# Converting the w_in slices by visits, and products (0,0) and (0,1) one visit later, in a fused retention and SiLU kernel

## The chip, the cores and the metric

The kernel runs on one core of a Trainium2 chip. The metric is device time in microseconds from the first to the last of the program on that core; a time shown is the median of several runs. The engines of the core named here are TensorE (PE, with its weight loads as PEld), VectorE (DVE), ScalarE (ACT), GpSimd (POOL) and SyncE (SP), whose queue issues nearly all DMA transfers of this kernel. Each engine works through its own instructions in order.

## The reference

A recurrent retention layer feeds a two-layer network with SiLU. B=4, H=8, S=768, D=64; 3072 tokens of 512 numbers; w_in is 512 x 2048 and w_out 2048 x 512, both 64-bit floats.

```python
gamma = 1.0 - 2.0 ** (-5.0 - np.arange(H))
for t in range(S):
    state = gamma * state + outer(k[:, :, t], v[:, :, t])      # per batch and head, D x D
    y[:, :, t] = scale * q[:, :, t] @ state
x = y.transpose(0, 2, 1, 3).reshape(B * S, H * D)
h = x @ w_in
out = (h / (1 + exp(-h))) @ w_out
```

## The kernel before

**Chunks and units.** The sequence is cut into NC=6 chunks c of 128 steps; with the 4 batches b that makes 24 units n = 4c+b. Inside a chunk, retention is a masked product of scores; between chunks a state (D x D per head) is carried. `visit(m)` (L497) works on three units at once: it transposes k and q of unit m (`stage_t`, L353, with ACT copying the results out of PSUM), forms the scores and state sums of unit m-1 (`stage_s`, `stage_a`), and the output y of unit m-2 (`stage_y`, L409). On DVE `finish_a` (L390) multiplies the scores by the decay mask ("am", L394) and updates the state (L403, L407), `scale_q` (L348) and `scale_k` (L330) scale q and k; for units 8 to 13 k's scaling is done on ACT in two halves of four heads. `finish_y` (L445) copies y out (L454) and `split_x` (L459) cuts it into three parts of limited precision for PE: the first on ACT (L466), two on DVE (L469, L470).

**Products.** `product_in(c, f)` (L535) multiplies chunk c's x (512 columns, four units) by slice f of w_in (128 of its 2048 columns): 8 matrix instructions into "ha", 4 into "hb". ACT copies ha out (L543), DVE subtracts hb (L547), ACT applies Silu (L551), and `put_g` (L554) sends the result g to DRAM one product later. The three PSUM banks "h" that hold ha and hb are shared with the transposes of k. Copies of y and the g tiles share three buffers "hs".

**Slices of w_in.** A slice arrives as 64-bit words (`load_w`, L153, two buffers "wf"). `convert_w` (L172) turns it into 32-bit numbers: one ACT instruction (L193) and six on DVE (L195 to L210, the last in `rounded`). `split_w` (L111) cuts the result into three parts: ACT (L117), DVE (L120), ACT (L122), DVE (L123). `take_w` (L218) does this for the next slice in number; with parts=1 the end of it is put behind the subtraction of the next product (list `behind_next`), with parts=2 the conversion and the first step of `split_w` are put there and the remaining three steps behind the mask of the next visit (list `behind_mask`, emptied in `visit`). Converting slice i also asks for the load of slice i+2, which waits until slice i's buffer has been read.

**What sets the order.** The order on PE is the order of the program, written out by hand at the end of the kernel (L608 to L662). The order on the other engines, and that of SP's transfers, is made when the kernel is built, by a planner that goes by priority (place in the program) and by its own estimate of when each instruction is ready; `tc.issue_after(x)` makes the instructions in its block follow x on x's engine. `taken_out[0]` is the latest product's subtraction, `masked[0]` the latest mask, `copied[0]` the latest copy of ha, `evac[0]` the latest copy of transposed k or q. Once a first product has run, `finish_a` is put behind `taken_out[0]` (in `visit`).

**The order before, around the change.** Visits 0 to 3; slice 0 taken; visits 4 and 5; slice 1 taken behind visit 5's mask; visit 6; product (0,0); visit 7; the load of slice 3; visit 8; product (0,1); slice 2 taken with parts=2; visit 9. Then the list `steps`: (1,0), visit 10, (1,1), visit 11, (0,2), (1,2), visit 12, (0,3), (1,3), visit 13, (0,4), (1,4), (2,0), (0,5) and so on. The slices 3 to 9 are taken after (1,0), (0,2), (0,3), (0,4), (0,5), (0,6), (0,7).

Exp is used on ACT for the decays of `chunk_decays` and `first_chunk` at visit 0; its first Silu is that of product (0,0).

Of the kernel before, what the change touches and what calls it, by code (L numbers as in the profile page):

```python
# [15 lines left out]
AF = mybir.ActivationFunctionType  # L16
# [15 lines left out]
def kernel(  # L32
# [27 lines left out]
    nc = tc.nc  # L60
    B, H, S, D = q.shape
# [11 lines left out]
    scale = 1.0 / math.sqrt(D)  # L73
# [37 lines left out]
    def split_w(f, w32, name, factor, to):  # L111


        to[f] = w = w_slot(f, name)
        lo = conv.tile([128, 512], FP32, tag="wl", name=f"{name}l_{f}")
        with tc.issue_after(held[0] if f >= NF - 4 else evac[0]):
            nc.scalar.activation(out=w[:, 0, :], in_=w32, func=AF.Copy, scale=HALF * factor)  # L117
        high = w[:, 0, :].bitcast(FP32)
        yield
        nc.vector.scalar_tensor_tensor(out=lo, in0=w32, scalar=factor, in1=high,  # L120
                                       op0=ALU.mult, op1=ALU.subtract)
        nc.scalar.activation(out=w[:, 1, :], in_=lo, func=AF.Copy, scale=1.0 / EPS)  # L122
        nc.vector.scalar_tensor_tensor(out=w[:, 2, :], in0=high, scalar=EPS, in1=lo,  # L123
                                       op0=ALU.mult, op1=ALU.subtract)
# [4 lines left out]
    EARLY = 2 * B  # L129
    early = {}  # L130

    def load(name, n):
        if n >= len(units):
            return
        c, b = units[n]
        src = {"k": k, "q": q, "v": v}[name]
        if n < EARLY:

            if n not in early:
                early[n] = wpool.tile([128, 3, H, D], FP32, tag=f"w{4 + n}", name=f"kqv_{n}")  # L140
            t = early[n][:, "kqv".index(name)]
        else:
            t = ld.tile([128, H, D], FP32, tag=f"{name}f", name=f"{name}f_{n}",
                        bufs=2 if name == "q" else 3)
        nc.sync.dma_start(out=t, in_=src[b, :, ds(c * C, C)].rearrange("h t d -> t h d"))  # L145
        kqv[name][n] = t
# [68 lines left out]
    evac, held, w_sb = [], [], {}  # L215
    taken = [0]

    def take_w(after=None, parts=0):  # L218


        i = taken[0]
        taken[0] += 1
        if i >= 2 * NF:
            return
        with tc.issue_after(after) if after else ExitStack():
            rounded = convert_w(i)

        def finish():
            w32 = rounded()
            if i < NF:  # L230
                split = split_w(i, w32, "wi", scale, w_sb)
                if parts == 2:
                    next(split)
                    behind_mask.append(split)
                else:
                    list(split)
            else:
                nc.sync.dma_start(out=wo_dram[i - NF], in_=w32)

        if parts:  # L240
            behind_next.append(finish)
        else:
            with tc.issue_after(after) if after else ExitStack():
                finish()

    W_AHEAD = 2
    for n in range(EARLY):
# [17 lines left out]
    for j in range(2):  # L265
        for a in range(HP):
            nc.scalar.activation(out=decay[:, j, a, :], in_=lag[:, :D], func=AF.Exp,
                                 scale=float(lg[2 * a + j]))
# [5 lines left out]
    lgc = const.tile([128, HP], FP32, tag="lgc", name="lgc")  # L274
# [16 lines left out]
    def first_chunk():  # L291
        nc.gpsimd.iota(lag, pattern=[[1, C]], base=1, channel_multiplier=0,
                       allow_small_or_imprecise_dtypes=True)
        for a in range(HP):
            nc.scalar.activation(out=gq[:, a, :], in_=lag, func=AF.Exp, scale=lgc[:, a : a + 1])

    def next_chunk():
        for a in range(HP):
            nc.scalar.activation(out=gq[:, a, :], in_=gq[:, a, :], func=AF.Copy,
                                 scale=step[:, a : a + 1])  # L300


    xt, kt, qt, am = {}, {}, {}, {}
    behind_next, behind_mask, behind_copy = [], [], []
    taken_out, copied, masked = [], [], []
    state, steps_of = {}, {}

# [13 lines left out]
    token = const.tile([1, 1], FP32, tag="token", name="token")  # L321
# [8 lines left out]
    def scale_k(n):  # L330
        if 0 <= n < len(units):
            t = kqv["k"][n]
            if units[n][0] == NC - 1:
                t = t[:D]
            if 2 * B <= n < 3 * B + 2:

                def half(heads):
                    for h in heads:
                        nc.scalar.activation(out=t[:, h, :], in_=t[:, h, :], func=AF.Copy,
                                             scale=gk[:, units[n][0], h : h + 1])  # L340

                half(range(H // 2))
                behind_copy.append(lambda: half(range(H // 2, H)))
                return
            g = gk[: t.shape[0], units[n][0], :].unsqueeze(2).to_broadcast([t.shape[0], H, D])
            nc.vector.tensor_tensor(out=t, in0=t, in1=g, op=ALU.mult)
# [150 lines left out]
    def visit(m):  # L497

        first, mid, last = (0 <= m - i < len(units) for i in range(3))
        if first:  # L500
            stage_t(m)
        if last:
            scores, states_with, yp = stage_y(m - 2)
            scores()
        if mid:
            sc, sums = score_tile(m - 1)
            stage_s(m - 1, sums)
        if last:
            states_with(0)
        if mid:  # L510
            stage_a(m - 1, sc)
            if m > 1 and units[m - 1][1] == 0:
                next_chunk()
            with tc.issue_after(taken_out[0]) if taken_out else ExitStack():
                finish_a(m - 1, sc, sums)
            with tc.issue_after(masked[0]):
                while behind_mask:
                    list(behind_mask.pop(0))
            scale_q(m - 1)
        if m == 0:  # L520
            chunk_decays()
            first_chunk()
        if first:
            scale_k(m)
        if last:
            states_with(1)
            finish_y(m - 2, yp)
        for name, n in (("k", m + 2), ("q", m + 2), ("v", m + 1)):
            if n >= EARLY:
                load(name, n)  # L530


    pending = []

    def product_in(c, f):  # L535
        ha, hb = turn(f"ha_{c}_{f}"), turn(f"hb_{c}_{f}")
        for i in range(3):
            for kk in range(KIN):
                nc.tensor.matmul(hb if i == 2 else ha, lhsT=w_sb[f][:, i, ts(kk, 128)],  # L539
                                 rhs=xt[c][:, i, kk, :], start=kk == 0 and i != 1,  # L540
                                 stop=kk == KIN - 1 and i != 0)
        hs = hpool.tile([128, NT], FP32, tag="hs", name=f"g_{c}_{f}")
        copied[:] = [nc.scalar.activation(out=hs, in_=ha, func=AF.Copy, scale=ONE_E).ins]  # L543
        with tc.issue_after(copied[0]):
            while behind_copy:
                behind_copy.pop(0)()
        taken_out[:] = [nc.vector.tensor_tensor(out=hs, in0=hs, in1=hb, op=ALU.subtract).ins]  # L547
        with tc.issue_after(taken_out[0]):
            while behind_next:
                behind_next.pop(0)()  # L550
        nc.scalar.activation(out=hs, in_=hs, func=AF.Silu)  # L551
        pending.append((c, f, hs))
# [55 lines left out]
    for m in range(EARLY + 2):  # L608
        visit(m)
        if m == 3:  # L610
            take_w()
        elif m == 5:
            take_w(masked[0])
        elif m == EARLY - 2:
            product_in(0, 0)
        elif m == EARLY - 1:
            load_w(3)
        elif m == EARLY:
            product_in(0, 1)
            take_w(taken_out[0], 2)  # L620

    half = NF // 2
    pairs = [(1, 0), (1, 1)] + [(c, f) for f in range(2, 4) for c in range(2)]
# [4 lines left out]
            [(2, f) for f in range(half, NF)])  # L628
    groups = [(c, f) for c in range(3, NC) for f in range(NF)]
    steps = pairs + three + rest + last + groups  # L630
    takes = [(1, 0)] + [(0, f) for f in range(2, half)]
    takes += [(2, half - 4), (2, half - 2)]
    takes += [(0, half), (0, half + 2), (1, half), (1, half + 2)]
    takes += [(0, NF - 4), (0, NF - 2), (2, half + 2), (2, half + 4)]
    takes += [(c, f) for c in (3, 4) for f in (0, 3, 6, 8, 11, 14)]
    behind = {(1, f): lambda f=f: visit(EARLY + 2 + f) for f in range(4)}
    at = ([(1, NF - 1)] + [(2, f) for f in range(NF - 7, NF - 2, 2)] +
          [(c, 4 * i + 1) for c in range(3, NC - 1) for i in range(B)])
    for i, x in enumerate(at):
# [5 lines left out]
    for n, (c, f) in enumerate(steps):  # L645
        product_in(c, f)
        if (c, f) in takes:
            take_w(taken_out[0], 2 if n < len(pairs) else int(n < len(pairs + three)))
        put_g(1)
        behind.get((c, f), lambda: None)()  # L650
        if c == NC - 1:
            if f == 0:
                get_w(0)
                get_w(1)
            if f < NF - 4:
                w_out(f)
            if f >= NF - 6:
                if f == NF - 6:
                    for n in range(G_AHEAD):
                        get(n)  # L660
                if f >= NF - S_AHEAD:
                    split(f - NF + S_AHEAD)  # L662
    put_g(0)

    for c in range(NC):
# [8 lines left out]
        for f in range(NF):  # L674
            n = c * NF + f
# [62 lines left out]
```

## Time and profile before

| | us |
|---|---|
| median of 6 runs (636.47 to 640.79) | 639.14 |
| the profiled execution's own time | 640.48 |
| its span | 638.7 |
| PE busy in the span | 612.9 |
| DVE busy | 421.7 |
| ACT busy | 305.2 |

The profile is one execution. Its page gives totals, slices of the span and the costliest groups; the trace behind it can be asked for stretches of time (busy time of each engine, granted TensorE clock, share of the DMA engines), for what each engine waited for, and for the instructions in order of time. A row in order of time reads: start, duration, engine, line, operation, output<-input. Durations overlap a little: a 128x512 instruction on DVE shows 0.68 or 0.69 us, and the next starts 0.60 us after it began. Times in microseconds are from the start of the span.

### The profile page before, as it was taken

Reading aid. Unit: us, or ns where it says so; the run is one execution under the profiler, and the core shown is the slowest. Engines: PE = TensorE matmul, PEld = TensorE weight load, DVE = VectorE, ACT = ScalarE, POOL = GpSimd, SP = SyncE. Lnnn points to the kernel's source line nnn. Section 1 sums busy time; section 2 is a strip of 40 time slices with the busy share of each in tenths; the row PEclk is TensorE's granted clock in tenths of the full one; section 3 lists DMA queues with packets and bytes.
Section 4 is the critical chain, followed back from the end, with each engine's and each line's share of the span. In section 5 each row is a group of like instructions: output and inputs, shape, how many; then the busy total and the mean of one; then the engine's idle time right before and its main releaser. Section 6 shows DMA issues by size and latency. Waiting matters only on the chain.

```text
span 638.7 us, 13560 instructions
## 1 busy us (share of the span) xinstructions
PE 612.9 (96%) x5440; PEld 507.1 (79%) x5440; DVE 421.7 (66%) x731; ACT 305.2 (48%) x590; POOL 7.3 (1%) x65
## 2 busy tenths in 40 slices
PE   5787999999999999999999999999999999999997
PEld 4676888887888888888887788888888888888785
DVE  2896899798977778687777766363544645554631
ACT  5675997666755555555467762231412221312311
POOL 3000000000000000000000000000000000000000
PEclk9998999999999999999999999999999999999999
DMA  9995877554677677774756643242342524332301
GB/s 202 204 218 121 225 211 240 173 165 158 208 214 186 195 239 214 211 232 166 231 192 214 201 153 107 91 166 98 133 131 78 186 67 132 132 123 88 120 0 67
DMA packets 123215, 103.65 MB, mean 162 GB/s; under 512 B 80016, under 2 KB 88464, under 8 KB 123152
## 3 DMA queue, kind: packets, MB, share of 16 engines
q1 hardware_dynamic: 120272, 97.54, 51.9%
q10 hardware_dynamic: 2880, 5.24, 2.2%
q8 instruction: 43, 0.70, 0.5%
q14 instruction: 20, 0.16, 0.1%
HBM read 66.06 MB, written 36.70 MB: 161 GB/s over the span
## 4 chain that ended last, share of the span: by engine, by line
PE 84%; DMA 4%; DVE 4%; ACT 3%; SPq 2%; issue 2%; ACTq 0%; DVEq 0%; POOLq 0%
PE ha L539 23%; PE o L687 20%; PE oa L687 13%; PE hb L539 12%; PE ob L687 7%; PE y L419 3%; DMA wf<-in_moe_w_in_dram 1%; DMA wr<-wod 1%; PE sc L376 1%; PE sc L386 1%; SPq L145 1%; PE qp L360 1%; PE kp L360 1%; DMA kqv<-in_q_dram 1%; DMA kf<-in_k_dram 1%
## 5 line engine op out<-in xcount | busy, mean ns | idle before, releaser
L539 PE MATMUL ha<-xt,wi 128*128 128x512 f32 x768 | 194.5, 396 | 1.8 <-ACT xt L466 1.8
L539 PEld LDWEIGHTS ha<-xt,wi 128*128 128x128 f32 x768 | 143.4, 189 | 33.1 <-ACT xt L466 2.0
L687 PE MATMUL o<-wo,gs 128*128 128x512 f32 x576 | 146.3, 389 | 0.0
L687 PEld LDWEIGHTS o<-wo,gs 128*128 128x128 f32 x576 | 108.2, 188 | 22.4
L596 DVE TENSOR_TENSOR gs<-gr,gs 128x512 fp32r<-128x512 f32 x96 | 62.2, 686 | 90.7 <-ACT gs L594 90.7
L687 PE MATMUL oa<-wo,gs 128*128 128x512 f32 x384 | 118.3, 389 | 0.0
L594 ACT ACTIVATE gs<-gr 128x512 fp32r<-128x512 f32 x96 | 53.4, 620 | 134.7 <-issue 132.3
L539 PE MATMUL hb<-xt,wi 128*128 128x512 f32 x384 | 104.6, 395 | 2.1 <-ACT g L543 2.1
L547 DVE TENSOR_TENSOR g<-g,hb 128x512 f32<-128x512 f32 x96 | 65.7, 685 | 46.4 <-ACT g L543 27.3
L539 PEld LDWEIGHTS hb<-xt,wi 128*128 128x128 f32 x384 | 72.9, 191 | 18.9 <-ACT g L543 3.5
L687 PEld LDWEIGHTS oa<-wo,gs 128*128 128x128 f32 x384 | 72.1, 188 | 15.0
L551 ACT ACTIVATE g<-g 128x512 f32<-128x512 f32 x96 | 60.7, 632 | 46.9 <-DVE g L547 46.5
L687 PE MATMUL ob<-wo,gs 128*128 128x512 f32 x192 | 75.3, 392 | 0.3 <-DVE o L696 0.3
L543 ACT ACTIVATE g<-ha 128x512 f32<-128x512 f32 x96 | 56.7, 591 | 35.7 <-PE ha L539 23.9
L597 DVE SCALAR_TENSOR_TENSOR gs<-gs 128x512 fp32r<-128x512 f32 x96 | 62.0, 685 | 0.0
L687 PEld LDWEIGHTS ob<-wo,gs 128*128 128x128 f32 x192 | 36.1, 188 | 9.3 <-DVE o L696 2.0
L193 ACT ACTIVATE ca<-wf 128x512 f32<-128x512 f32 x32 | 21.7, 677 | 11.1 <-DVE cs L200 5.1
L419 PE MATMUL y<-qt,mid 64*64 64x64 f32 x384 | 21.4, 226 | 2.1 <-issue 2.1
L394 DVE TENSOR_TENSOR am<-sc,decay 128x512 f32<-128x512 f32 x24 | 16.5, 687 | 9.9 <-PE sc L386 9.9
L200 DVE SCALAR_TENSOR_TENSOR cs<-ca,cs 128x512 uint32<-128x512 uint32 x32 | 22.1, 691 | 1.0
L204 DVE SCALAR_TENSOR_TENSOR cp<-wf,cp 128x512 f32<-128x512 uint32 x32 | 22.1, 690 | 0.7
L695 ACT ACTIVATE o<-o 128x512 f32<-128x512 f32 x10 | 6.0, 597 | 33.4 <-PE o L687 33.0
(79 smaller groups left out, 539.1 us busy)
## 6 DMA issues: line engine op xcount, KB each, us to landing
gd<-g SPq DMA_DIRECT2D x96, 256.0 KB, 3.1
gr<-gd SPq DMA_DIRECT2D x96, 256.0 KB, 2.7
wf<-in_moe_w_out_dram SPq DMA_DIRECT2D x16, 512.0 KB, 4.2
out_dram<-o ACTq DMA_DIRECT2D x20, 256.0 KB, 2.1
wf<-in_moe_w_in_dram SPq DMA_DIRECT2D x16, 256.0 KB, 4.2
wf<-in_moe_w_in_dram SPq DMA_DIRECT2D x32, 128.0 KB, 3.9
kf<-in_k_dram SPq DMA_DIRECT2D x16, 256.0 KB, 5.3
qf<-in_q_dram SPq DMA_DIRECT2D x16, 256.0 KB, 4.1
```

What stands on the lines that cost most here:

```text
L193: nc.scalar.activation(out=a.bitcast(FP32), in_=hi.bitcast(FP32), func=AF.Abs, scale=65536.0)
L200: nc.vector.scalar_tensor_tensor(out=s, in0=a, scalar=3, in1=s, op0=ALU.logical_shift_left, op1=ALU.bitwise_or)
L204: nc.vector.scalar_tensor_tensor(out=p.bitcast(FP32), in0=lo, scalar=2.0 ** -52, in1=p.bitcast(FP32), op0=ALU.mult, op1=ALU.mult)
L419: i = nc.tensor.matmul(yp[ts(e, D), o, a, :], lhsT=lhsT, rhs=rhs, start=(e, o) not in started, stop=True, skip_group_check=True).ins
L539: nc.tensor.matmul(hb if i == 2 else ha, lhsT=w_sb[f][:, i, ts(kk, 128)], rhs=xt[c][:, i, kk, :], start=kk == 0 and i != 1, stop=kk == KIN ...
L543: copied[:] = [nc.scalar.activation(out=hs, in_=ha, func=AF.Copy, scale=ONE_E).ins]
L547: taken_out[:] = [nc.vector.tensor_tensor(out=hs, in0=hs, in1=hb, op=ALU.subtract).ins]
L551: nc.scalar.activation(out=hs, in_=hs, func=AF.Silu)
L594: nc.scalar.activation(out=t[:, 0, :], in_=g, func=AF.Copy, scale=HALF)
L596: nc.vector.tensor_tensor(out=t[:, 1, :], in0=g, in1=high, op=ALU.subtract)
L597: nc.vector.scalar_tensor_tensor(out=t[:, 2, :], in0=t[:, 1, :].bitcast(FP32), scalar=-1.0 / EPS, in1=high, op0=ALU.mult, op1=ALU.add)
L687: nc.tensor.matmul(o, lhsT=g, rhs=wo[f][:, i, :], start=first_ and i != 1, stop=last and i != 0)
```

## The change

Slice 1 is converted from visit 6 and no longer from visit 5, and slices 2 to 6 from visits 8, 10, 11, 12 and 13 (`begin_w`, in `visit`, behind that visit's mask): the conversion and the first step of `split_w`. The remaining three steps (`end_w`) follow the mask of the next visit, or, for slice 6, the subtraction of the product after visit 13. Slices 7 and on are taken as before, so `take_w` needs no third kind of `parts`. `finish_a` is put behind the latest subtraction only for visits after 13. Products (0,0) and (0,1) follow visits 7 and 9; (0,0) still precedes visit 8 and (0,1) now directly precedes (1,0). The k of unit 8 is scaled by DVE in one instruction, no longer by ACT in eight. After the Exps of `first_chunk` a Silu of one element is added, whose result is not used.

```diff
-                split = split_w(i, w32, "wi", scale, w_sb)
-                if parts == 2:
-                    next(split)
-                    behind_mask.append(split)
-                else:
-                    list(split)
+                list(split_w(i, w32, "wi", scale, w_sb))
...
+    def end_w():
+        while half_split:
+            list(half_split.pop())
+
+    def begin_w():
+        i = taken[0]
+        taken[0] += 1
+        split = split_w(i, convert_w(i)(), "wi", scale, w_sb)
+        next(split)
+        half_split.append(split)
...
+        nc.scalar.activation(out=token, in_=lgc[:1, :1], func=AF.Silu)
...
-            if 2 * B <= n < 3 * B + 2:
+            if 2 * B < n < 3 * B + 2:
...
-            with tc.issue_after(taken_out[0]) if taken_out else ExitStack():
+
+            with tc.issue_after(taken_out[0]) if m > 3 * B + 1 else ExitStack():
                 finish_a(m - 1, sc, sums)
-            with tc.issue_after(masked[0]):
-                while behind_mask:
-                    list(behind_mask.pop(0))
             scale_q(m - 1)
...
+        if EARLY - 2 <= m < 3 * B + 2:
+            with tc.issue_after(masked[0]):
+                end_w()
+                if m not in (EARLY - 1, EARLY + 1):
+                    begin_w()
...
-        elif m == 5:
-            take_w(masked[0])
-        elif m == EARLY - 2:
-            product_in(0, 0)
         elif m == EARLY - 1:
             load_w(3)
-        elif m == EARLY:
+            product_in(0, 0)
+        elif m == EARLY + 1:
             product_in(0, 1)
-            take_w(taken_out[0], 2)
...
-    takes = [(1, 0)] + [(0, f) for f in range(2, half)]
+    takes = [(0, f) for f in range(5, half)]
...
-    behind = {(1, f): lambda f=f: visit(EARLY + 2 + f) for f in range(4)}
+    behind = {(1, f): lambda f=f: visit(EARLY + 2 + f) for f in range(3)}
+    behind[1, 3] = lambda: [visit(3 * B + 1), behind_next.append(end_w)]
...
-            take_w(taken_out[0], 2 if n < len(pairs) else int(n < len(pairs + three)))
+            take_w(taken_out[0], n < len(pairs + three))
```

EARLY is 8, B is 4 and `half` is 8.

## The prediction

> **What bounds the kernel now.** I read the page's totals first, then a table of stretches, the waits of one stretch, and the order of work on each engine from 33 to 100 us. PE is busy for 612.9 of 638.7 us, so only a pause of PE costs time. In the table of stretches the columns after the length are busy time and count of PE, weight loads, VectorE (DVE), ScalarE (ACT) and POOL, then granted clock, DMA share and GB/s.
>
> ```profile
> 42.00:44.00 2.00, 1.71 (x52) 1.40 (x44) 2.00 (x5) 1.76 (x3) 0.09 (x1) 1.00 0.74 154
> 44.00:46.00 2.00, 0.23 (x14) 0.25 (x17) 2.00 (x5) 1.99 (x4) 0.00 (x0) 1.00 0.85 209
> 46.00:48.00 2.00, 1.52 (x104) 1.39 (x98) 1.97 (x4) 2.00 (x7) 0.00 (x0) 1.00 0.92 235
> 48.00:50.00 2.00, 0.62 (x39) 0.48 (x30) 1.81 (x5) 0.71 (x2) 0.09 (x1) 1.00 0.95 182
> 50.00:52.00 2.00, 1.30 (x5) 1.04 (x6) 0.35 (x2) 0.96 (x2) 0.00 (x0) 0.90 1.01 225
> 52.00:54.00 2.00, 2.00 (x6) 1.51 (x6) 1.38 (x2) 1.13 (x4) 0.00 (x0) 0.50 0.21 46
> ...
> 58.00:60.00 2.00, 0.63 (x28) 0.36 (x20) 1.97 (x5) 1.97 (x7) 0.20 (x1) 1.00 0.40 93
> 60.00:62.00 2.00, 1.45 (x6) 1.23 (x7) 1.97 (x4) 0.50 (x1) 0.00 (x0) 0.96 0.54 166
> 62.00:64.00 2.00, 2.00 (x6) 1.51 (x6) 0.08 (x1) 0.69 (x2) 0.00 (x0) 0.50 0.81 217
> ```
>
> At 44 to 46 us DVE and ACT are full and PE nearly empty; from 52 to 54 and 62 to 64 us PE is full but at half clock. What ended PE's pauses from 36 to 66 us (waiter, what it waited for; total, times, longest):
>
> ```profile
> PE y L419 <- issue: 2.1, 1, 2.1
> PE y L419 <- ACT ys L454: 2.1, 1, 2.1
> PE ha L539 <- ACT xt L466: 1.8, 1, 1.8
> PE sc L376 <- DVE state L407: 0.5, 1, 0.5
> ```
>
> Why they are there stands in the order on DVE and ACT:
>
> ```profile
> 43.13 0.68 DVE L123 SCALAR_TENSOR_TENSOR wi<-wi,wil 128x512 fp32r<-128x512 f32 x1
> 43.74 0.68 DVE L547 TENSOR_TENSOR g<-g,hb 128x512 f32<-128x512 f32 x1
> 44.33 0.69 DVE L346 TENSOR_TENSOR kqv<-kqv,gk 128x512 f32<-128x512 f32 x1
> 44.94 0.69 DVE L394 TENSOR_TENSOR am<-sc,decay 128x512 f32<-128x512 f32 x1
> ...
> 43.31 1.28 ACT L551 ACT_TABLE_LOAD   x1
> 44.60 0.63 ACT L551 ACTIVATE g<-g 128x512 f32<-128x512 f32 x1
> 45.14 0.57 ACT L454 COPY ys<-y 128x512 f32<-128x512 f32 x1
> ```
>
> Unit 6's scores leave PE at 42.40; their mask starts 2.5 us later, behind the end of slice 1's conversion and behind product (0,0)'s subtraction, which the before kernel forces. On ACT the table load and the Silu stand ahead of the copy of y. PE can't go on until 45.77. From 60.6 to 97.9 us PE is busy 36.5 of 37.3 us and DVE hardly idles, so there both are close to the bound.
>
> **The change part by part.** The sum goes against the profiled execution: 640.48 us, span 638.7; the median of the runs is 639.14, 1.34 below it.
>
> *Products (0,0) and (0,1) one visit later.* No instruction is added. Before, PE runs visit 6 to 36.35, (0,0) to 39.21, visit 7 to 42.6, visit 8 to 50.9, (0,1) to 55.35, visit 9 to 58.7, and (1,0) starts at 60.55, having waited 1.84 for ACT to finish the x of visit 9. With (0,1) between visit 9 and (1,0), 2.72 us of product (its length at full clock, 76.82 to 79.54) cover that wait: 1.84 gone. For (0,0): visit 7 starts at 36.35 instead. Its k and q landed at 30.29+4.9=35.2 and 31.12+5.1=36.2, so it isn't starved; visit 7 takes about 3.1 us (as 79.54 to 82.6 does) and 0.8 of waits named below, (0,0) 2.72: visit 8 would start near 42.9, with q8 in at 36.76+5.3=42.1, visit 9 3.1 later, near 46, with q9 in at 39.53+5.7=45.2, v8 at 46.0. The queue of loads (SP) stays just ahead. The copies of y gain a buffer: a g tile of (0,0) holds one of three "hs" buffers a visit less.
>
> *Early masks free of the subtraction; slice 1 converted from visit 6 instead of 5.* Slice 1's conversion is 3 DVE instructions of 0.34 and 5 of 0.60 start to start: 4.05 us, and three of ACT, 1.65. Today it runs from 35.45 to 43.8 between the work of visits 5 to 7. Behind the mask, it leaves visit 7's path; the mask of unit 6 can start as PE ends the scores. PE's waits for y (2.06) and state (0.48) go. What is late next: DVE stands at 34.84 with x of visit 6 (0.72+0.60) and k of unit 6 (0.60) ahead, so the mask of unit 5 starts near 36.8 and its state (0.60+0.33+0.60 on) near 38.3, done at 38.7; PE, at y from 37.2 and at the sums from 38.1, waits about 0.3+0.5; by the same reckoning visit 9 waits about 0.7 for its state: 1.5 given back.
>
> *Early Silu.* The table load takes 1.28 (row above) on ACT ahead of the copy of y; it moves to about 8.8 us, where ACT's next copy for PE has slack until DVE's mask at 12.57, itself held by a slice's DMA at 12.23. Added: one 1-element Silu, about 0.2 (the 128x1 rows of L281 are 193 ns). Worth nothing of its own beyond the 2.06 counted. If that cover is gone it costs up to 1.5; if the planner puts it among the Exps, two more loads, 2.6, partly hidden by visit 2's wait for its inputs at 13 us: bounds 0 to +2.6, taken 0.
> [...]
>
> *The clock.* The granted clock of the 2 us stretches puts the half clock at 51.6 to 55.0 and 61.8 to 65.2 us, each behind a pause (2.08 and 1.84 us); the pause of 2.06 from 43.7 us brought none, so where a pause falls counts too. (0,1) takes 4.54 us and (1,0) 4.43 against 2.72: 3.53 lost. Bounds: all or none of it returns; with two of the three pauses gone I take all.
> [...]
>
> *The 2.08 us put down to "issue"* (48.6 to 50.7, in the last product of visit 8): the trace shows no releaser. It may stay whole or go with the order; bounds 0 and 2.08, taken half, 1.04.
>
> *Slices 2 to 6 by visits 8 to 13, 7 on as before.* The same instructions; each starts behind its visit's mask, and its last three follow the next visit's mask instead of a subtraction. Slice 2 begins a product earlier, 6 before (0,4) instead of after it. SP: slice 4's load now stands in visit 8 and waits for slice 2's buffer (the L204 row), with the loads of visit 9 behind it; before, one such wait ran beside 6.1 us of waiting for q's buffer, ended by visit 9's transposes at 56; they come near 46.8 now. If that L204 runs at 54 to 57 us, k11 lands 2.4 (the issues ahead of it) and 3.4 us later, at 59.8 to 62.8, for visit 11 near 61.7: bounds 0 and 1.1, taken 0, the other end in the range. POOL's fences move with the visits and wait for PE alone.
>
> *k of unit 8 scaled by DVE instead of ACT.* 8 ACT instructions of 0.25 (2.0 us) leave ACT, one of 0.60 joins DVE. Bounds -2.0 and +0.6; DVE is the fuller one (20.1 of 24.3 us busy from 36.3 to 60.6, ACT 17.6), so I take +0.6.
>
> Sum on PE: 2.06+0.48+2.08+1.84+3.53=9.99 lost now; less 1.5 and 1.04 it leaves 7.5. But DVE then limits: between 34.84 and 100.28 us (subtraction of (2,0)) its gaps of 0.19 us or more, read from its order, are 0.24+0.19+1.93+1.91+3.00+1.19+0.40=8.86. With 0.60 added at most 8.3 can be taken out. That leaves no room for waits of a conversion on its own ACT step (0.4 to 0.7 each in the rows of L120); for three or so of them I take 2 us. 8.3-2.0=6.3, under 7.5, so 6.3 it is: 634.2 for the profiled execution, 632.8 for the median. From 100 us on PE runs back to back to 151.7, and the DVE has gaps of 0.5 to 1.1 per product: what is won before it stays won.
>
> **Rivals.**
> (a) DVE and ACT as the bound give most back. For: DVE is full in nine tenths of 70 to 100 us and six conversions lie there. Against: the same conversions are there now. If the clock still halves once (1.77) and all six conversions wait 0.6 on ACT (3.6, instead of 2.0), the gain is 6.3-1.77-1.6=2.9: 636.2.
> (b) It does next to nothing: the inputs are the limit. For: DMA share is 0.9 to 1.1 until 48 us, and my visits 8 and 9 start only 0.8 us after their q. Against: all of visit 10's inputs were issued by 50.3 us and land by 55. If wf of slice 3, waiting for slice 1's buffer until 45 instead of 42.9, drags k10 and q10 by 2 us and slice 4's wait drags k11 by 3 more, 6.3-5=1.3 us of gain remain: 637.8.
> (c) Slower: a conversion started in the middle of each visit on an in-order DVE sits ahead of the state and of the next mask. Its first part is 2.82 us (3x0.34+3x0.60). For: today the interleaved slice 1 is exactly what delayed visit 7. Against: it begins after the mask. If it adds a wait of PE in visits 8 and 10 to 13 it decides from 6.3/5=1.3 us a visit; at 1.9 each, two thirds of the part, 9.5-6.3=+3.2: 639.14+3.2=642.3.
>
> **How the numbers follow.** 0.3% is 1.9 us, about what a measurement of this kernel can tell. Main case, gains of 4 to 9.6 (629.5 to 635.1): 0.56. (a), gains of 1.9 to 4: 0.20. (b): 0.08, of which 0.06 within 0.3%. (c): 0.16, of which 0.02 within 0.3%. So faster 0.56+0.20+0.02=0.78, within 0.06+0.02=0.08, slower 0.14. Range: the best case recovers 9.99 but 0.4, 629.5; the upper end holds (a), (b) and 2.0 us more, from the table loads' 2.6 and the queue's 1.1: 637.8+2.0=639.8. Left out is nearly all of (c).
>
> **What would show it.** Right: between 36 and 56 us no PE wait over 1 us for ys or xt, (1,0) starting near 53 to 55 us instead of 60.55, granted clock 1.00 throughout 50 to 66, one table load before 11 us, (2,0) ending 5 to 8 us earlier than 100.9. Wrong: PE waits for state or kf in visits 8 to 13, SP waits on cp L204 with k loads behind them, more than two table loads, or DVE without a gap to 100 us and PE with several.

## The result, and the profile after

| | before | after |
|---|---|---|
| median, us | 639.02 (47 runs) | 635.34 (21 runs) |
| lowest to highest | 636.06 to 642.91 | 633.70 to 636.47 |
| profiled execution, span | 640.48, 638.7 | 635.57, 633.8 |

The ratio is 0.994, 95% interval 0.9928 to 0.9953: 3.7 us by the medians, where 6.3 were forecast. The range (629.5 to 639.8) and the direction held; the main case (gains of 4 to 9.6) did not, the gain lies in rival (a)'s band, and the runs below show another reason for it than (a)'s.

The table of stretches of the kernel after, the rows that were shown of before (length; busy time and count of PE, weight loads, DVE, ACT, POOL; granted clock, DMA share, GB/s):

```profile
42.00:44.00 2.00, 2.00 (x11) 1.59 (x10) 2.00 (x5) 0.50 (x1) 0.00 (x0) 1.00 1.21 211
44.00:46.00 2.00, 2.00 (x77) 1.83 (x79) 2.00 (x5) 1.06 (x3) 0.00 (x0) 1.00 0.77 174
46.00:48.00 2.00, 1.10 (x71) 0.97 (x64) 2.00 (x4) 1.94 (x5) 0.09 (x1) 1.00 0.82 238
48.00:50.00 2.00, 1.24 (x9) 0.86 (x8) 2.00 (x5) 1.39 (x4) 0.00 (x0) 1.00 1.14 234
50.00:52.00 2.00, 1.33 (x73) 1.22 (x77) 2.00 (x6) 2.00 (x6) 0.00 (x0) 1.00 1.02 176
52.00:54.00 2.00, 1.07 (x63) 0.89 (x56) 1.97 (x5) 1.60 (x7) 0.17 (x1) 1.00 0.33 76
...
58.00:60.00 2.00, 1.90 (x9) 1.22 (x8) 2.00 (x5) 1.51 (x4) 0.00 (x0) 1.00 1.02 274
60.00:62.00 2.00, 2.00 (x41) 1.46 (x43) 1.14 (x2) 1.48 (x4) 0.00 (x0) 1.00 0.17 54
62.00:64.00 2.00, 1.02 (x67) 0.90 (x60) 0.00 (x0) 2.00 (x7) 0.09 (x1) 1.00 0.38 133
```

PE no longer stands empty at 44 us, and the half clock at 52 and 62 us is gone. But PE has new holes, from 46 to 54 and at 62 to 64 us. What ended PE's pauses from 36 to 66 us after:

```profile
PE y L428 <- issue: 2.2, 2, 1.3
PE sc L395 <- issue: 1.1, 1, 1.1
PE sc L385 <- DVE state L416: 0.7, 2, 0.5
PE y L428 <- DVE am L403: 0.6, 1, 0.6
```

The waits for the copy of y (2.1) and for x (1.8) are gone; "issue", time in which PE waited for nothing that the profile shows, is now 3.3 us of the 4.6, where it was 2.1 of 6.5.

The order on DVE and ACT after, around the subtraction of (0,0):

```profile
48.16 0.69 DVE L559 TENSOR_TENSOR g<-g,hb 128x512 f32<-128x512 f32 x1
48.75 0.70 DVE L355 TENSOR_TENSOR kf<-kf,gk 128x512 f32<-128x512 f32 x1
49.36 0.69 DVE L403 TENSOR_TENSOR am<-sc,decay 128x512 f32<-128x512 f32 x1
...
48.88 0.63 ACT L563 ACTIVATE g<-g 128x512 f32<-128x512 f32 x1 [0.61 <-DVE g L559]
49.42 0.57 ACT L463 COPY ys<-y 128x512 f32<-128x512 f32 x1
```

The subtraction and unit 8's k are still ahead of a mask, now unit 7's, whose scores left PE at 46.8; no table load precedes the Silu. By PE's order of work the gain builds up so: (1,0) starts at 57.20 instead of 60.55, (1,1) at 64.99 instead of 68.06, (0,2) at 70.90 instead of 73.96. So 3.1 of the profile's 4.9 us come from ahead of (1,1), 0.7 is given back until 101 us, 1.5 more come at 150 us, where PE waited 1.26 for ACT before and does not after, and the last 1.0 later, nearly all of it at 342 and 354 us, where PE waited 0.49 and 0.33 for ACT before. The 1.5 at 150 us do not belong to the order: a second profile of the changed kernel has a wait of 1.0 there, and the profiles of the products alone and the masks alone, which keep the old order of slices, have none. So of this pair's 4.9 us some 2.4 are won up to 101 us, and the pair can't be read as the medians' 3.7 split into places.

### The profile page after: what moved, and what is told of

It is laid out like the page before. It is cut to its first block, busy times and chain, and to the rows that moved or that the text cites. A ratio compares the mean times of both kernels' runs of the same rounds, so it can differ in the third digit from the quotient of the medians.

```text
span 633.8 us, 13555 instructions
## 1 busy us (share of the span) xinstructions
PE 611.6 (97%) x5440; PEld 506.2 (80%) x5440; DVE 421.1 (66%) x732; ACT 303.2 (48%) x583; POOL 7.2 (1%) x65
## 4 chain that ended last, share of the span: by engine, by line
PE 84%; SPq 5%; DVE 4%; ACT 3%; DMA 3%; issue 1%; ACTq 0%; DVEq 0%; POOLq 0%
PE ha L551 25%; PE o L696 20%; PE oa L696 14%; PE hb L551 13%; PE ob L696 7%; SPq L145 4%; PE y L428 2%; DMA yd<-ys 1%; PE sc L385 1%; PE sc L395 1%; DMA kf<-in_k_dram 1%; PE kp L369 1%; PE qp L369 1%; ACT kf L348 1%; DMA kqv<-in_q_dram 1%
## 5 line engine op out<-in xcount | busy, mean ns | idle before, releaser
L551 PE MATMUL ha<-xt,wi 128*128 128x512 f32 x768 | 192.5, 393 | 0.0
L551 PE MATMUL hb<-xt,wi 128*128 128x512 f32 x384 | 103.3, 391 | 0.4 <-ACT g L555 0.2
L563 ACT ACTIVATE g<-g 128x512 f32<-128x512 f32 x96 | 60.6, 631 | 49.3 <-DVE g L559 49.1
L555 ACT ACTIVATE g<-ha 128x512 f32<-128x512 f32 x96 | 56.8, 591 | 32.4 <-PE ha L551 22.8
```

## The experiments

Ratios are to the kernel before on the same chip. All profiles are of one execution each, and their waits differ from one to the next more than the medians do.

### The parts alone

**Products alone.** Four heads of unit 8's k are scaled only behind (0,1) here, after visit 9 has used them, so part of that unit's state is left unscaled; number and kinds of instructions are those of the kernel before.

```diff
-        elif m == EARLY - 2:
-            product_in(0, 0)
         elif m == EARLY - 1:
             load_w(3)
+            product_in(0, 0)
         elif m == EARLY:
-            product_in(0, 1)
             take_w(taken_out[0], 2)
+        elif m == EARLY + 1:
+            product_in(0, 1)
```

> The kernel before with products (0,0) and (0,1) one visit later, nothing else. My theory (PE waited for x and y behind DVE and ACT): the 1.84 us wait of (1,0) goes and with it one half-clock window, 1.7; the mask of unit 6 stands free of the subtraction of (0,0) by order alone. 2 to 4 us faster, near the whole of the change. The rival (PE runs out of instructions: the waits put down to issue move and grow as visits follow each other without a product between): the 1.84 goes but issue waits in visits 8 to 10 rise from 2.1 to 3.3 or more; 0 to 2 us faster.

Measured: 638.29 us, ratio 0.9993 (0.9971 to 1.0015): no change that can be told. What ended PE's pauses from 36 to 66 us in it:

```profile
PE y L419 <- issue: 2.7, 2, 1.4
PE sc L376 <- DVE state L407: 1.3, 2, 0.8
PE y L419 <- ACT qt L362: 1.2, 1, 1.2
PE y L419 <- DVE qt L351: 0.5, 1, 0.5
...
```

The 1.8 us wait for x is gone, as both theories said, and no half clock follows, as mine said (the mean granted clock is 1.00 from 36 to 66 us), and still nothing is won. Slice 1's eight DVE instructions stand between the masks, states and q of visits 6 and 7 (36.76 to 45.1 us), PE waits for states and q there, and issue waits rise from 2.1 to 2.7, not to the rival's 3.3.

**Slices alone**: the changed kernel with products, masks, Silu and unit 8's k as before.

> The kernel before with slices 1 to 6 begun by visits and ended behind the next mask, nothing else. My theory: slice 1 leaves the DVE ahead of visit 7, but the subtraction of (0,0) still stands ahead of the mask of unit 6 and the table load ahead of the copy of y: 0.5 to 2 us faster. The rival (issue waits decide): within 1 us, either way, with the 2.1 us issue wait in visit 8 still there.

Measured: 637.60 us, 0.9971 (0.9954 to 0.9988), about 1.9 us of the gain by the ratio. The issue wait in visit 8 is there, at 2.05 us, and (1,0) waits 2.2 for x:

```profile
PE ha L550 <- ACT xt L474: 2.2, 1, 2.2
PE y L427 <- issue: 2.0, 1, 2.0
PE y L427 <- ACT ys L462: 1.5, 1, 1.5
```

**Masks alone, Silu alone.**

```diff
-            with tc.issue_after(taken_out[0]) if taken_out else ExitStack():
+            with tc.issue_after(taken_out[0]) if m > 3 * B + 1 else ExitStack():
...
+        nc.scalar.activation(out=token, in_=lgc[:1, :1], func=AF.Silu)
```

> The kernel before with early masks free of the subtractions, nothing else. My theory: the mask of unit 6 starts up to 1.2 us sooner (two instructions of 0.60 no longer ahead), but the copy of y behind the table load ends PE's wait at the same place: 0 to 0.7 us faster. The rival: no change beyond 0.3 us.

> The kernel before with the early Silu alone. My theory: the copy of y starts up to 1.3 us sooner, but unit 6's mask, done at 45.6 us, ends PE's wait: 0 to 0.3 us faster, two table loads in all, the second near 8.9 us. The rival (the load was on the path): 1.0 to 1.3 us faster.

Measured: 1.0003 (0.9983 to 1.0024) and 0.9998 (0.9975 to 1.0020). Neither tells from no change. In the Silu's run the order on ACT is

```profile
7.51 1.26 ACT L295 ACTIVATE gq<-lag,lgc 128x128 f32<-128x128 f32 x4
8.79 1.28 ACT L297 ACT_TABLE_LOAD   x1
10.08 0.20 ACT L297 ACTIVATE token<-lgc 1x1 f32<-1x1 f32 x1
10.19 0.56 ACT L364 COPY kt<-kp 128x512 f32<-128x512 f32 x1
```

so it stands behind all the Exps, and PE's wait in visit 8 is still 1.9 us, now put down to unit 6's mask: the copy of y and the mask were late together, and taking one away leaves the other:

```profile
PE y L421 <- DVE am L396: 1.9, 1, 1.9
```

The parts add up to -0.07-0.29+0.03-0.02 = -0.35%; the whole is -0.6%. Each part is known to about 0.2%, so the sum alone does not show that some count only together; the next runs bear on that. Unit 8's k, the fifth part of the change, was not tried by itself.

### Parts taken out of the whole

**Products back behind visits 6 and 8.**

```diff
-        elif m == EARLY - 1:
+        elif m == EARLY - 2:
+            product_in(0, 0)
+        elif m == EARLY - 1:
             load_w(3)
-            product_in(0, 0)
-        elif m == EARLY + 1:
+        elif m == EARLY:
             product_in(0, 1)
```

> The changed kernel with products (0,0) and (0,1) back behind visits 6 and 8. Theory now (VectorE is the bound from 34 to 61 us, and the products' new place counts only where slice 1 is out of visit 7's way): (1,0) waits about 1.9 us for x again, and half clock follows; 1.5 to 2.5 us slower than the changed kernel, ratio to before near 0.997, as the slices alone gave. Rival (the parts add up: products alone gave 0.9993): less than 0.6 us slower, ratio near 0.995.

Measured: 636.98 us, 0.9976 (0.9959 to 0.9994), beside 0.994 (0.9928 to 0.9953) of the whole; 1.6 us slower by the medians. The wait for x is back:

```profile
PE ha L551 <- ACT xt L475: 2.2, 1, 2.2
PE y L428 <- issue: 1.2, 1, 1.2
PE y L428 <- ACT ys L463: 1.1, 1, 1.1
...
```

The products' new place is thus worth about 0.3% once slice 1 is out of visit 7's way; alone it showed 0.07%, known to about 0.2%. The slices alone gave 0.9971 and differ from this run by masks, Silu and unit 8's k: with the products in their old place these three together show nothing that can be told.

The execution profiled took 634.90 us, where the median is 636.98, so the 1.6 us are not to be looked for in it, and that the expected half clock didn't follow is true of this execution only. The issue waits are 1.4 us in this stretch, 0.2 of it at the scores, against 3.3 in the changed kernel. The other profiles agree: from 36 to 66 us the five with the products behind visits 6 and 8 have 0.7 to 2.1 us of issue waits, the six with them behind visits 7 and 9 (PE's instructions not shifted) 2.7 to 5.8. With products between the visits there are fewer.

**Without the early Silu, and without Silu and free masks.**

```diff
-        nc.scalar.activation(out=token, in_=lgc[:1, :1], func=AF.Silu)
...
-            with tc.issue_after(taken_out[0]) if m > 3 * B + 1 else ExitStack():
+            with tc.issue_after(taken_out[0]) if taken_out else ExitStack():
```

> The changed kernel without the early Silu: the table load (1.28 us) stands before the Silu of (0,0) at about 48 us, ahead of the copy of y, in a stretch in which ScalarE is busy 8 tenths. Theory now (VectorE binds there): 0 to 0.5 us slower than the changed kernel. Rival: 1 to 1.3 us slower.

> The changed kernel without the early Silu and with the masks behind the subtractions again, so products and slices only (and unit 8's k on VectorE). Theory now: these two make the whole of the change; ratio 0.994 to 0.995. Rival (the table load and the masks matter once the rest is out of the way): the table load stands ahead of the copy of y in visit 8 or 9, 1.3 us, ratio 0.996 or more.

Measured: without the Silu 636.38 us, 0.9967 (0.9951 to 0.9983); without both 636.32 us, 0.9957 (0.9938 to 0.9976). Both intervals overlap the whole's. By the medians both are about 1 us slower than the changed kernel (by the ratios 1.7 and 1.1); the interval of the first only just overlaps the whole's, and the second, which lacks the Silu too, is no slower. What the two are worth, between 0 and somewhat over 1 us, stays open.

**(0,1) behind visit 8, (0,0) where the change has it.**

```diff
-        elif m == EARLY + 1:
+        elif m == EARLY:
             product_in(0, 1)
```

> The changed kernel with product (0,1) back behind visit 8. My theory of the prediction (the product covers the x of visit 9 for (1,0)): (1,0) waits 1.8 us again, 1.5 to 2 us slower than the changed kernel. Theory of the code: with a product between visits 8 and 9 one issue wait of about 1 us goes, so 0.5 to 1 us slower only.

Measured: 636.63 us, 0.9959 (0.9937 to 0.9981); the changed kernel in the same batch 635.75, 0.9948 (0.9924 to 0.9971). In its profile, of an execution of 638.09 us, (1,0) waits 3.3 us for x:

```profile
PE ha L551 <- ACT xt L475: 3.3, 1, 3.3
```

Yet the median is only 0.9 us longer, with overlapping intervals: it speaks for the second theory's 0.5 to 1 and settles little.

### What "issue" is

**The changed kernel again, and with PE's instructions shifted.**

```diff
+    pad = banks("q", "pad", 1)[:, 0]
+    for i in range(32):
+        nc.tensor.matmul(pad[:D, ts(i % 8, D)], lhsT=ident[:D, :D], rhs=ident[:D, :D],
+                         start=True, stop=True, skip_group_check=True)
     for m in range(EARLY + 2):
```

> The changed kernel as it is, for a second profile and as the mate of the next three. If the late start of visit 6 (33.65 us against 32.78) and the half clock from 30.5 us belong to this order, they are here again; if they come from how fast the inputs land in one execution (q of unit 5 took 5.7 us from issue, 4.2 in the profile before), they differ. If the waits put down to issue come from the order of PE's instructions, they stand in the same instructions: visits 8, 9, 10 and 13, 4.4 us in all.

> The changed kernel with 32 small matrix products on the identity, 64 instructions, put ahead of visit 0 on PE, while it waits for the first inputs; their result is not used. Theory of the code: PE's instructions come in blocks of some 250, and a visit uses up its block before the next has come; the issue waits move by 64 instructions, to other places in the visits, and their sum changes (1 to 6 us). Rival (the waits belong to the last products of a visit, or to their weights): they stay in the same instructions with the same 4.4 us, and the time is within 0.5 us.

> As the run before with 64 products, 128 instructions, half a block. Theory of the code: the issue waits move by half a block, so those that fell at the end of a visit fall near its middle or into a product, where 24 instructions last 2.7 us and cover the fetch; sum 1 to 6 us, another one than with 64 instructions. Rival: same places, same 4.4 us.

Each product is two matrix instructions and two weight loads on PE (the trace has 64 and 128 matrix instructions), so the shifts are 128 and 256 instructions, half a block and a whole one by the count of 253 below, and take 7.08 and 13.91 us. By the theory of the code it is then the second, planned as half a block, that must put the waits back where they were. Measured: 635.75, 635.95 and 642.14 us; 0.9948 (0.9924 to 0.9971), 0.9942 (0.9915 to 0.9969) and 1.0058 (1.0027 to 1.0089).

In order of time, the issue waits of the changed kernel's first profile (in brackets, ahead of the instruction that ended them):

```profile
48.38 0.21 PE L428 MATMUL y<-qt,mid 64*64 64x64 f32 x1 [1.28 <-issue]
...
53.94 0.21 PE L428 MATMUL y<-qt,state 64*64 64x64 f32 x1 [0.93 <-issue]
...
64.14 0.63 PE L395 MATMUL sc<-qt,kt 64*64 64x64 f32 x27 [1.12 <-issue]
```

In the second profile of the same kernel:

```profile
36.57 0.21 PE L428 MATMUL y<-am,kqv 64*64 64x64 f32 x1 [1.17 <-issue]
...
42.44 0.38 PE L428 MATMUL y<-am,kqv 64*64 64x64 f32 x9 [2.52 <-issue]
...
55.76 0.21 PE L428 MATMUL y<-qt,state 64*64 64x64 f32 x1 [0.61 <-issue]
...
66.56 0.63 PE L395 MATMUL sc<-qt,kt 64*64 64x64 f32 x27 [1.40 <-issue]
```

With half a block more:

```profile
37.67 0.50 PE L395 MATMUL sc<-qt,kt 64*64 64x64 f32 x17 [0.58 <-issue]
...
43.54 0.62 PE L395 MATMUL sc<-qt,kt 64*64 64x64 f32 x26 [2.28 <-issue]
...
55.16 0.39 PE L385 MATMUL sc<-vf,kf 64*64 64x64 f32 x10 [0.86 <-issue]
```

With a whole block more:

```profile
45.79 0.38 PE L428 MATMUL y<-am,kqv 64*64 64x64 f32 x9 [0.50 <-issue]
...
53.89 0.21 PE L428 MATMUL y<-qt,mid 64*64 64x64 f32 x1 [0.28 <-issue]
...
61.23 0.26 PE L428 MATMUL y<-qt,state 64*64 64x64 f32 x1 [0.77 <-issue]
```

The second profile answers its expectation in part: visit 6 is late again (33.69 us), the half clock at 30.5 us is not there, the waits of visits 9, 10 and 13 stand in the same instructions, but the one of visit 8 is gone, and visits 6 and 7 have two new ones; 6.4 us in all instead of 4.4. Its execution took 637.84 us, the longest of its ten.

Half a block moves the waits to other instructions of the visits; a whole block puts them back to ones that the two profiles above have (nine products with the masked scores left in visit 7, the last product of visit 8, one near the end of visit 9). The rival, that they belong to certain instructions, falls. And in each of these cases the instruction queue moved one block (0.70 MB in 43 by the rows further down, 16 KB each) shortly before. In the changed kernel it has one transfer in each of the stretches 45.7 to 46.7, 51.1 to 52.4 and 61.5 to 62.9 us (count, MB, share):

```profile
q8 instruction: 1, 0.02, 5.5%
...
q8 instruction: 1, 0.02, 5.7%
...
q8 instruction: 1, 0.02, 5.8%
```

Measured from the start of the transfer in the trace (45.76, 51.15 and 61.52 us), PE goes on 2.62, 2.79 and 2.62 us later in the changed kernel, 2.58 in the kernel before (transfer at 48.12, PE at 50.70), 2.58 with the half block's shift (40.96, 43.54), and 3.68 in the second profile, where the transfer took 2.24 us; most take 0.9 to 1.5. The 14 profiles have 61 issue waits up to 110 us. In 58 of them PE goes on 2.25 to 3.11 us after a transfer began, in two 3.34 and 3.68 us after one that took 1.90 and 2.24 us; one, of 0.48 us with the whole block's shift, has no transfer near it. The pages of the changed kernel and of the one with a whole block more count

```profile
q8 instruction: 43, 0.70, 0.5%
...
q8 instruction: 44, 0.72, 0.5%
```

That is one transfer per 253 of the 10,880 instructions of PE, and one more for 256 more. That the queue is PE's, and that PE had run out of code where it has an issue wait, is my inference from these counts, the shifts and the steady delay; no row of the profile names it.

A visit uses up 272 instructions, more than such a block, in about 3 us (136 matrix instructions and 136 weight loads, 3.06 us from 79.54 to 82.60 before), and where a wait shows in these four profiles it is 0.3 to 2.5 us.

The run with the whole block tells one thing more: visit 0 begins 11.3 us later (15.30 instead of 4.03), visit 6 6.2 later (39.84 instead of 33.65), and the median 6.4 later than its mate's 635.75. So 5.1 us of the delay are made up by visit 6: until then PE waits 3.5 us for the DMA of k and q in the changed kernel, and not at all in this run. Behind visit 6 nothing is made up.

### Is VectorE the bound?

Slice 2 is ready some 11 us before it is needed (its last step on DVE ends at 59.85 us, (0,2) starts at 70.90), and DVE idles 3.5 us at 61 to 65 us. So I moved it there:

```diff
-                if m not in (EARLY - 1, EARLY + 1):
+                if m not in (EARLY - 1, EARLY, EARLY + 1):
                     begin_w()
...
+        if (c, f) == (1, 0):
+            behind_next.append(begin_w)
         product_in(c, f)
```

> The changed kernel with slice 2 begun behind the subtraction of (1,0), and no longer in visit 8; slice 2 is needed 13 us after it is ready now, and VectorE then idles 3.5 us. Theory (VectorE is the bound from 34 to 61 us): 4.05 us of its work leave that stretch for the idle one, (1,0) no longer waits 0.6 us for x, the subtractions of (0,1) and (1,0) come earlier: 0.5 to 1.5 us faster than the changed kernel. Rival (PE's own code and the inputs set the pace there): within 0.4 us.

Measured: 636.06 us, 0.9956 (0.9937 to 0.9975), no faster than the changed kernel. The stretch from 50 to 61 us, first of the changed kernel, then of this one:

```profile
50.00:61.00 11.00, 9.30 (x156) 7.12 (x157) 10.71 (x22) 8.63 (x22) 0.17 (x1) 1.00 0.73 174
```

```profile
50.00:61.00 11.00, 9.72 (x172) 8.17 (x170) 6.97 (x13) 9.26 (x25) 0.09 (x1) 1.00 0.78 184
```

DVE went from 10.71 to 6.97 us busy, and all of PE's waits from 36 to 66 us were then

```profile
PE y L428 <- issue: 4.3, 3, 1.6
```

So with DVE's load taken off, (1,0) still starts at 57.29 (57.20 in the changed kernel): the waits for DVE are gone (1.3 us in the changed kernel) and the issue waits are 4.3 us instead of 3.3, in these two executions. (1,1) is 1.6 us ahead there, at 63.41; a wait of 0.85 for a subtraction at 76 us gives half of that back. No version of these beats the changed kernel.

## Why the prediction was right and wrong

- **Products one visit later.** Right that the 1.84 of (1,0) goes and that the products now hide the x of visit 9. Wrong in counting it on its own: alone it won nothing that can be told, with the slices about 0.3%. My visit 7 at 36.35 came at 37.14 in the profile after (37.1 to 38.3 in six other runs with this order up to there), visit 9 at 48.53 for "near 46", (1,0) at 57.20 for "53 to 55"; (2,0) ended 2.4 us earlier than before, at 98.55, not 5 to 8.
- **Masks and slice 1.** Right that the 2.06 for y goes. The waits of 1.5 that I gave back for masks and states measured 0.24+0.58+0.47 = 1.3. Slices alone carry half of the gain. The masks' freedom, which I named in the same step, showed nothing by itself.
- **Early Silu.** Right at nothing of its own, and at its place (8.87 us, behind the Exps).
- **The clock.** The half clock at 52 and 62 us is gone, as taken. This seems to belong to the order: from 36 to 66 us the mean granted clock is 0.83, 0.89, 0.89, 0.94 and 1.00 in the five profiles with the products in their old places, and 1.00 in five of the six with them in the new ones (0.94 in the second profile of the changed kernel). The 3.53 were mis-sized a little: from start to start the two products took 4.45 and 4.23 us, 3.24 more than two at full clock. And not all came back: one half clock stands at 30.5 to 33.9 us in the profile after, as it does near there in the profiles of the products, the slices and the masks alone, and one at 43.5 in its second; with slice 2 late there is none from 18 to 631 us, and the time is the same.
- **The 2.08 put down to "issue".** This is the term that was wrong, in size and in kind. I took half of it to stay, 1.04, with bounds 0 and 2.08. Measured in the same stretch: 3.3 us in the profile after, 4.3 in its second. It is a price of visits without a product between them (0.7 to 2.1 us in five profiles, 2.7 to 5.8 in six), and the change strings visits 6 and 7, and 8 and 9, together. With 3.3 or 4.3 in its place the sum on PE is 5.2 or 4.2 instead of 7.5. That is below the 6.3 of DVE, so PE's own waits would have set the forecast, nearer to the 3.7 measured by the medians. That this term is the whole of the shortfall is argued from the sum; no run took the issue waits away and nothing else.
- **The ceiling of DVE.** The 6.3 came from this term. In the profile after DVE is full from 36 to 60 us, but then has a gap of 3.5 up to visit 10's scores, in which PE has an issue wait of 1.1, and freeing 4 us of DVE moved nothing. So it was not what set the gain. Nor did DVE hardly idle from 60.6 to 97.9 us before: it was busy for 32.4 of 37.3 us.
- **Rivals.** (a) had the size (2.9 us) but not the reason: no wait of a conversion on ACT shows among PE's. (b): up to visit 6 PE does wait for inputs, 3.5 us in the profile after, but from 36 to 66 us no wait for a DMA shows. (c): from visit 7 on PE waited no more than 0.6 us for a state or mask at a time in the profile after.
- **Not predicted:** 1.5 us at 150 us, where ACT waited 2.84 us for a slice's DMA in the profile before and 0.98 after. It belongs to the execution and not to the order: the second profile of the changed kernel waits there too, and two profiles with the old order of slices do not.

## What to carry to other kernels

A pause that the profile puts down to nothing should be looked up against the transfers of the instruction queue before it is called chance: here, where visits of 272 instructions in about 3 us follow each other, the issue waits from 36 to 66 us were 2.7 to 5.8 us, and with a product of 24 instructions that lasts 2.7 us between them 0.7 to 2.1. Moving such long work away, to cover another wait, can cost what it wins. Two things that are late together (here the mask and the copy of y) each gain nothing when only one of them is taken away, so parts tried one by one can add up to less than the whole. And two profiles of one execution each can differ by pauses that no change made (here 1.5 us at 150 us): a pause is worth looking up in the other profiles before it is put down to the change.

## What was unexpected of the hardware

- In 58 of 61 issue waits PE goes on 2.25 to 3.11 us after a 16 KB transfer of the instruction queue began (3.68 in one where the transfer took 2.24 us), and the same program has issue waits of 4.4 and 6.4 us in two executions.
- The clock halved at 30.5 us after no single pause over 1.1 us, in an execution with several (1.06, 1.08, 0.42, 1.01 us between 23 and 30 us), and at 43.5 us, in the second profile of that kernel, after one of 2.52. The three half clocks within the work in the profiles before and after last 3.41 us each. In the 3.41 us ahead of them PE was busy for 1.34 us (48.17 to 51.59, before), 1.58 (58.41 to 61.83, before) and 1.98 (27.09 to 30.50, after). In the two stretches of that length around the pause of 2.06 us before it was busy for 2.24 and 1.93 us (from 41.35 and from 44.76), and no half clock followed. So the longest pause does not tell when one comes, and the busy time in such a stretch leaves no sharp limit: 1.98 had one behind it, 1.93 none. What sets it is not shown here.
- A delay of 11.3 us at the start cost 6.4 at the end.
